# Decode attention over two caches: PV on four column groups, and V in one slot of a whole tile

## The chip, the cores and the metric

The kernel runs on one core of one Trainium2 chip. The metric is the device time of one execution in microseconds (us); several executions are timed, and the median counts. A profile is one more execution with the hardware profiler on.

## The reference

Two independent attention layers decode one token each and are joined side by side. Both have 32 heads of 128 and a cache of 16384 positions; layer A attends to all of them, layer B to the last 4096.

```python
q = (x @ wq).reshape(1, 1, 32, 128).transpose(0, 2, 1, 3)
k, v = k_cache, v_cache                      # B: only [:, :, Sk - 4096 :, :]
scores = einsum("bhqd,bhkd->bhqk", q, k) * 128 ** -0.5
o = einsum("bhqk,bhkd->bhqd", softmax(scores), v)
out = o.transpose(0, 2, 1, 3).reshape(1, 1, 4096) @ wo     # wo: 4096 x 512
return concatenate([out_A, out_B], axis=-1)                # 1 x 1 x 1024, bf16
```

x is 1 x 512, wq 512 x 4096, everything in bf16. A's K and V are 134 MB each, B's windows 33.5 MB each, the four weight matrices 4.2 MB each: 352 MB are read once.

## The kernel before

**Tiles.** A tile holds 8.39 MB of K: 128 partitions with 64 KB each. For A that is two heads: 64 partitions a head, 256 consecutive positions a partition. For B it is two groups of four heads (halves of a tile): a group has 32 partitions a head and 128 positions a partition. There are 20 tiles in a fixed list `steps`; B's are numbers 0, 7, 13 and 19, the rest are A's. T counts tiles, and a step is what the loop does for one tile; u is the half of a tile, CH = 128 positions.

**Scores on DVE.** `scores_prod` (L206) multiplies half a tile of K by q in place, 128 x 16384 elements. `scores_tree` folds the 128 products of a position with four additions (L213, 64 + 32 + 16 + 8 wide) and a reduction over the last 8 (L219) into `sc`. `unit_max` (L224, L226) takes the maximum per partition and turns it on PE; `max_all` (L231 to L238) takes the maximum per head and spreads it again over the partitions by a product on PE.

**Softmax on ACT.** `soft` makes the bias (L243), the exponentials with their sums (L246), and spreads p by head with a mask (L254), so that `pm` holds for four positions of a partition one column for each pair of head and position. `soft_sum` adds over the partitions on PE (L268, L273), `recip` inverts on DVE.

**PV on PE.** `pv` (L298): for each four positions of a partition one matmul with `pm` (128 x 8 for A, 128 x 16 for B) as weights and 128 x 512 of V as the moving operand. All add into the first 8 or 16 rows of one PSUM tile `o`; only the blocks where position meets position are wanted. `evict` scales by the reciprocal (L314, ACT), `columns` picks the wanted blocks with four small products (L329) and writes the heads' columns into `s.O` (L333). The last of A's tiles but one (`split`) and B's last tile use `pv_columns` instead (L344): V as weights, one matmul a position.

**Ends.** `project_q` (L183) makes q at the start. `permute_o` rearranges a side's columns, `project_out_rows` (L379) multiplies A's by wo, and `project_out_columns` (L393) B's, with wo in five pieces of 16, 8, 4, 3 and 1 rows.

**Order.** The schedule is written by hand; each engine runs its instructions in the order in which the program gives them. All large loads go through SP's queue in program order, and a load that waits for its slot holds those behind it. K has two slots of a whole tile (`kring`), V two of half a tile (`vring`, 32 KB a partition). At the start B's wq, half of K(0), A's wq, the other half and K(1) are loaded; the wq's sit in V's slots; x of both sides comes over ACT's queue into a corner of K's second slot. For half u of tile T the loop does this:

```python
if u == 0 and T >= 1:
    load_v(T - 1, 0)
    if T + 1 < NT:
        new_k(T + 1)
        load_k(T + 1)
```

then `columns`, `scores_prod(T, u)`, and where a softmax is due `max_all`, `soft` and `soft_sum`; for u == 0 then `pv(T - 2, 1)`, `load_v(T - 1, 1)` and `pv(T - 1, 0)`; then `scores_tree`, `recip`, `evict`, `unit_max`. So a tile's V is loaded during the next tile's scores, its first half ahead of K(T + 1) in SP's queue and its second half behind it, and the second half of PV runs a step later still. In the last two halves A's wo and B's last V go into K's free slot, B's wo into one of V's.

Of the kernel before, what the change touches and what calls it, by code (L numbers as in the profile page):

```python
# [25 lines left out]
def kernel(  # L26
# [26 lines left out]
    vring = ctx.enter_context(tc.tile_pool(name="vring", bufs=2))  # L53
# [4 lines left out]
    ps_o = ctx.enter_context(tc.tile_pool(name="ps_o", bufs=2, space=bass.MemoryType.PSUM))  # L58
# [5 lines left out]
    def vslot(name):  # L64
        return vring.tile([P, CH, DH], BF16, tag="vring", name=name)
# [9 lines left out]
    for s, n, x, wq, wo, nh in ((A, "A", A_x, A_wq, A_wo, 2), (B, "B", B_x, B_wq, B_wo, 4)):  # L75
        s.n, s.x, s.wq, s.wo, s.nh = n, x, wq, wo, nh
# [5 lines left out]
        s.rows = singles.tile([P, nh, 4], F32, tag=f"rows{n}", name=f"rows{n}")  # L82
# [42 lines left out]
    def load_v(T, u, dst=None):  # L125
        s, g = steps[T]
        V[T, u] = vslot("vt") if dst is None else dst
        if s is A:
            src = a_pair(A_v_cache, g)[:, u * CH : (u + 1) * CH, :].rearrange("p l d -> p (l d)")
        else:  # L130
            src = b_window(B_v_cache, 2 * g + u)
        nc.sync.dma_start(out=V[T, u][:, :, :].rearrange("p l d -> p (l d)"), in_=src)

    def load_wq(s):
        s.wq_t = vslot("wqt")
        nc.sync.dma_start(  # L136
            out=s.wq_t[:, :, :].rearrange("p a b -> p (a b)").rearrange("p (c f) -> p c f", c=KC),
            in_=s.wq.rearrange("(p c) f -> p c f", c=KC),
        )
# [9 lines left out]
    def make_masks(s):  # L149
        nc.vector.tensor_reduce(out=s.mask[:, :], in_=by_head(s, identf[:, :]), axis=AX.X, op=ALU.add)  # L150
        nc.vector.tensor_copy(s.rows[:, :, :], s.mask[:, :].unsqueeze(2).broadcast_to([P, s.nh, 4]))
# [22 lines left out]
    def project_q(s):  # L174
        wq = s.wq_t[:, :, :].rearrange("p a b -> p (a b)").rearrange(
# [13 lines left out]
    class Unit:  # L189
        def __init__(self, T, u):  # L190
            self.T = T
            self.s, g = steps[T]
            self.col = self.s.nh * g if self.s is A else self.s.nh * (2 * g + u)
            self.n = 2 * CH if self.s is A else CH
            self.rows = 4 * self.s.nh
            self.split = T == NT - 3
            self.last = self.split or T == NT - 1
            self.sc = one.tile([P, 2 * CH], F32, tag="sc", name="sc")

# [8 lines left out]
    def scores_tree(T, u):  # L208
        s, g = steps[T]
# [5 lines left out]
        if s is B or u == 0:  # L215
            units[T, u] = Unit(T, u)
        un = units[T, u if s is B else 0]
        c0 = u * CH if s is A else 0
        nc.vector.tensor_reduce(out=un.sc[:, c0 : c0 + CH], in_=k[:, :, 0:8], axis=AX.X, op=ALU.add)  # L219
        return un if s is B or u == 1 else None  # L220

    def unit_max(un):
        m = small.tile([P, 1], F32, tag="m", name="m")
        nc.vector.tensor_reduce(out=m[:, :], in_=un.sc[:, 0 : un.n], axis=AX.X, op=ALU.max)  # L224
        un.sm = ps_m.tile([P, 512], F32, tag="sm", name="sm")
        nc.tensor.transpose(un.sm[0:1, 0:P], m[:, :], identf[:, :])  # L226

    def max_all(un):
        s = un.s
        M = small.tile([1, 4], F32, tag="M", name="M")  # L230
        nc.vector.tensor_reduce(  # L231
            out=M[:, 0 : s.nh], in_=by_head(s, un.sm[0:1, 0:P]), axis=AX.X, op=ALU.max
        )
        Mr = one.tile([1, P], F32, tag="Mr", name="Mr")
        nc.vector.tensor_copy(  # L235
            by_head(s, Mr[:, :]), M[:, 0 : s.nh].unsqueeze(2).broadcast_to([1, s.nh, P // s.nh])
        )
        nc.tensor.matmul(un.sm[:, 128:129], lhsT=Mr[:, :], rhs=one_f[:, :], start=True, stop=True)  # L238

    def soft(un):  # L240
        s = un.s
        bias = small.tile([P, 1], F32, tag="bias", name="bias")
        nc.scalar.activation(out=bias[:, :], in_=un.sm[:, 128:129], func=ACT.Copy, scale=-inv)  # L243
        p = one.tile([P, 2 * CH], BF16, tag="p", name="p")
        cs = small.tile([P, 1], F32, tag="cs", name="cs")
        nc.scalar.activation(  # L246
            out=p[:, 0 : un.n], in_=un.sc[:, 0 : un.n], func=ACT.Exp, scale=inv, bias=bias[:, :],
            accum_out=cs[:, :],
        )
        un.cs = cs  # L250
        pm = small.tile([P, 4 * CH], BF16, tag="pm", name="pm")
        un.pm = pm[:, 0 : un.n * s.nh].rearrange("p (i h c) -> p i h c", h=s.nh, c=4)
        for j in range(s.nh):
            nc.scalar.activation(  # L254
                out=un.pm[:, :, j, :], in_=p[:, 0 : un.n].rearrange("p (i c) -> p i c", c=4),
                func=ACT.Copy, scale=s.mask[:, j : j + 1],
            )

        if un.last:
            un.csm = small.tile([P, 4], F32, tag="csm", name="csm")  # L260
            nc.scalar.activation(
                out=un.csm[:, 0 : s.nh], in_=s.mask[:, :], func=ACT.Copy, scale=un.cs[:, :]
            )

    def soft_sum(un):
        s = un.s
        if un.last:
            nc.tensor.matmul(  # L268
                un.sm[:, 136 : 136 + s.nh], lhsT=ones_col[:, :].broadcast_to([P, P]),
                rhs=un.csm[:, 0 : s.nh], start=True, stop=True,  # L270
            )
        else:
            nc.tensor.matmul(  # L273
                un.sm[0 : un.rows, 136:137], lhsT=s.rows[:, :, :].rearrange("p a b -> p (a b)"),
                rhs=un.cs[:, :], start=True, stop=True,
            )

    def recip(un):
        un.r = small.tile([P, 4], F32, tag="r", name="r")
        if un.last:  # L280
            nc.vector.reciprocal(un.r[:, 0 : un.s.nh], un.sm[:, 136 : 136 + un.s.nh])
        else:
            nc.vector.reciprocal(un.r[0 : un.rows, 0:1], un.sm[0 : un.rows, 136:137])  # L283

    ready = []

    def pv(T, u):
        s = steps[T][0]
        un = units[T, u if s is B else 0]
        if un.split and u == 1:  # L290
            pv_columns(un, V[T, u], u * CH // 4)
            return
        first, final = (True, True) if s is B or un.split else (u == 0, u == 1)
        if first:
            un.o = ps_o.tile([16, 512], F32, tag="o", name="o")
        i0 = u * CH // 4 if s is A else 0
        for i in range(CH // 4):
            nc.tensor.matmul(  # L298
                un.o[0 : un.rows, :],
                lhsT=un.pm[:, i0 + i, :, :].rearrange("p a b -> p (a b)"),  # L300
                rhs=V[T, u][:, 4 * i : 4 * i + 4, :],
                start=(first and i == 0),
                stop=(final and i == CH // 4 - 1),
            )
        if final and not un.split:
            ready.append(un)

    evicted = []

    def evict():  # L310
        while ready:
            un = ready.pop(0)
            un.osb = one.tile([16, 512], F32, tag="o4", name="o4")
            nc.scalar.activation(  # L314
                out=un.osb[0 : un.rows, :], in_=un.o[0 : un.rows, :], func=ACT.Copy,
                scale=un.r[0 : un.rows, 0:1],
            )
            evicted.append(un)
            if ready:
                columns()  # L320

    def columns():
        while evicted:
            un = evicted.pop(0)
            s, n = un.s, un.rows
            oc = ps_s.tile([P, 4], F32, tag="sp", name="oc")
            sel = identf[0:n, 0:n].rearrange("k (h c) -> k c h", c=4)
            for j in range(4):
                nc.tensor.matmul(  # L329
                    oc[:, 0 : s.nh], lhsT=un.osb[0:n, j * P : (j + 1) * P], rhs=sel[:, j, :],  # L330
                    start=(j == 0), stop=(j == 3),
                )
            nc.scalar.copy(s.O[:, un.col : un.col + s.nh], oc[:, 0 : s.nh])  # L333

    def evict_part(un):
        un.part = one.tile([16, 512], F32, tag="o4", name="o4p")
        nc.scalar.copy(un.part[0 : un.rows, :], un.o[0 : un.rows, :])

    def pv_columns(un, V_t, i0):
        s, n = un.s, un.rows  # L340
        part = getattr(un, "part", None)
        o = ps_o.tile([P, 4], F32, tag="o", name="ocol")
        for l in range(CH):
            nc.tensor.matmul(  # L344
                o[:, 0 : s.nh], lhsT=V_t[:, l, :], rhs=un.pm[:, i0 + l // 4, :, l % 4],
                start=(l == 0), stop=(part is None and l == CH - 1),
            )
# [182 lines left out]
```

## Time and profile before

| | |
|---|---|
| median of 3 runs | 827.29 us (827.22 to 827.47) |
| the profiled execution | 827.69 us, its span 825.8 us |
| DVE busy | 761.7 us, 92% |
| PE busy with matmuls / weight loads | 391.3 us / 173.0 us |
| ACT busy | 67.1 us |
| bytes read | 352.32 MB |

The span is what the profiler's records cover; the execution's own time lies 1.9 us above it. Lines such as L298 are lines of the kernel before. In the views, "idle before" is time in which an engine waited, and behind the arrow stands what ended the wait. A DMA view of a stretch counts the packets that the 16 DMA engines moved in it, the megabytes, and the packets' time as a share of 16 engines for the stretch's length. PE is matrix multiplication, PEld its weight loads, SPq the queue of the engine that issues the large loads.

### The profile page before, as it was taken

What the parts mean: (1) busy time and instruction counts of PE and PEld (TensorE: products, weight loads), DVE (VectorE), ACT (ScalarE), POOL (GpSimd) and SP (SyncE); (2) the same over time, 40 slices, a digit from 0 to 9 for tenths busy, and PEclk for the clock granted to TensorE, in tenths of its full rate; (3) what the DMA queues carried; (4) which work ended last, traced back from release to release, by engine and by line L of the source; (5) the groups of instructions that cost most, each with busy time, mean ns of one, the idle gap of its engine ahead of it and who ended that gap; (6) DMA issues with size and microseconds to landing.
All of it is one profiled execution on the core that took longest, in us unless ns stands there. A gap on an engine that the chain in (4) does not pass through costs nothing.

```text
span 825.8 us, 5009 instructions
## 1 busy us (share of the span) xinstructions
PE 391.3 (47%) x2107; PEld 173.0 (21%) x2107; DVE 761.7 (92%) x361; ACT 67.1 (8%) x194; POOL 0.7 (0%) x6
## 2 busy tenths in 40 slices
PE   3505062808172644537180817354553617181794
PEld 1201020303031212212030302121221203030444
DVE  1899999999999999999999999999999999999930
ACT  0111010101000001101010100010010101010120
POOL 0000000000000000000000000000000000000000
PEclk9766576868585858677675859585767767575685
DMA  9999999999999999999999999999999999999996
GB/s 383 436 432 445 423 448 417 447 416 439 432 427 432 429 436 429 439 424 438 424 443 422 445 418 430 437 427 441 421 443 424 447 417 447 416 432 432 426 432 287
DMA packets 10404, 352.64 MB, mean 427 GB/s; under 512 B 1163, under 2 KB 1294, under 8 KB 1550
## 3 DMA queue, kind: packets, MB, share of 16 engines
q1 hardware_dynamic: 10376, 352.33, 99.2%
q8 instruction: 16, 0.26, 0.1%
q14 instruction: 6, 0.05, 0.0%
q10 hardware_dynamic: 6, 0.00, 0.0%
HBM read 352.32 MB, written 0.00 MB: 427 GB/s over the span
## 4 chain that ended last, share of the span: by engine, by line
DVE 77%; DMA 20%; PE 2%; issue 1%; SPq 0%; ACT 0%; DVEq 0%
DVE kt L206 35%; DVE kt L213 34%; DMA kt<-in_A_k_cache_dram 10%; DVE sc L219 5%; DMA kt<-in_B_k_cache_dram 5%; DMA wot<-in_B_wo_dram 4%; DMA vt<-in_A_v_cache_dram 2%; PE o L298 1%; DVE m L224 1%; DVE Mr L235 1%; DVE M L231 0%; PE ocol L344 0%; DVE r L283 0%; SPq L136 0%; SPq L146 0%
## 5 line engine op out<-in xcount | busy, mean ns | idle before, releaser
L213 DVE TENSOR_TENSOR kt<-kt 128x8192 bf16<-128x8192 bf16 (+3 forms) x160 | 344.9, 2156 | 4.7
L298 PE MATMUL o<-vt,pm 128*8 128x512 bf16 (+1 forms) x1184 | 300.1, 420 | 0.8 <-DMA vt<-in_A_v_cache_dram 0.8
L206 DVE TENSOR_TENSOR kt<-kt,qA 128x16384 bf16<-128x16384 bf16 x32 | 277.5, 8672 | 3.1 <-DMA kt<-in_A_k_cache_dram 3.0
L298 PEld LDWEIGHTS <-pm 128*8 128x8 bf16 (+1 forms) x1184 | 110.2, 94 | 181.5 <-issue 60.8
L226 PE MATMUL sm<-identf,m 128*1 128x128 f32 x24 | 8.5, 355 | 199.6 <-DVE m L224 199.5
L238 PE MATMUL sm<-one_f,Mr 1*128 1x1 f32 x48 | 13.1, 340 | 177.2 <-DVE Mr L235 177.2
L206 DVE TENSOR_TENSOR kt<-kt,qB 128x16384 bf16<-128x16384 bf16 x8 | 69.5, 8684 | 14.6 <-DMA kt<-in_B_k_cache_dram 14.6
L219 DVE TENSOR_REDUCE sc<-kt 128x128 f32<-128x1024 bf16 x40 | 48.8, 1220 | 3.3 <-DVE kt L213 0.5
L238 PEld LDWEIGHTS sm<-one_f,Mr 1*128 1x128 f32 x48 | 11.1, 285 | 184.1 <-DVE Mr L235 183.7
L226 PEld LDWEIGHTS sm<-identf,m 128*1 128x1 f32 x24 | 1.9, 79 | 202.2 <-issue 193.3
L243 ACT ACTIVATE bias<-sm 128x1 f32<-128x1 f32 x24 | 4.1, 171 | 404.0 <-PE sm L238 403.9
L314 ACT ACTIVATE o<-o,r 8x512 f32<-8x512 f32 (+1 forms) x21 | 14.3, 679 | 158.0 <-PE o L298 158.0
L329 PE MATMUL oc<-identf,o 8*128 8x2 f32 (+1 forms) x168 | 22.0, 249 | 2.9 <-ACT o L314 2.9
L329 PEld LDWEIGHTS oc<-identf,o 8*128 8x128 f32 (+1 forms) x168 | 20.2, 186 | 10.4 <-issue 6.5
L254 ACT ACTIVATE pm<-p,maskA 128x256 bf16<-128x256 bf16 x32 | 14.5, 500 | 0.5
L183 PE MATMUL qp<-wqt,xbA 128*128 128x512 bf16 x32 | 8.8, 444 | 9.5 <-DMA wqt<-in_A_wq_dram 9.5
L183 PE MATMUL qp<-wqt,scratch 128*128 128x512 bf16 x32 | 10.0, 488 | 5.3 <-DMA wqt<-in_B_wq_dram 5.3
L359 DVE TENSOR_TENSOR OB<-ocol,r 128x4 bf16<-128x4 f32 x2 | 0.3, 163 | 13.1 <-PE ocol L344 13.1
L246 ACT ACTIVATE p<-sc,bias 128x256 bf16<-128x256 f32 (+1 forms) x24 | 11.3, 472 | 0.8
L333 ACT CAST OA<-oc 128x2 bf16<-128x2 f32 x15 | 2.4, 161 | 102.6 <-PE oc L329 102.6
L254 ACT ACTIVATE pm<-p,maskB 128x128 bf16<-128x128 bf16 x32 | 10.2, 390 | 0.3
L224 DVE TENSOR_REDUCE m<-sc 128x1 f32<-128x256 f32 (+1 forms) x24 | 9.0, 374 | 0.6
(69 smaller groups left out, 98.6 us busy)
## 6 DMA issues: line engine op xcount, KB each, us to landing
vt<-in_A_v_cache_dram SPq DMA_DIRECT2D x32, 4096.0 KB, 26.5
kt<-in_B_k_cache_dram SPq DMA_DIRECT2D x8, 4096.0 KB, 35.3
vt<-in_B_v_cache_dram SPq DMA_DIRECT2D x7, 4096.0 KB, 33.2
wqt<-in_B_wq_dram SPq DMA_DIRECT2D x1, 4096.0 KB, 12.6
wqt<-in_A_wq_dram SPq DMA_DIRECT2D x1, 4096.0 KB
wot<-in_A_wo_dram SPq DMA_DIRECT2D x1, 4096.0 KB
wot<-in_B_v_cache_dram SPq DMA_DIRECT2D x1, 4096.0 KB, 29.3
wot<-in_B_wo_dram SPq DMA_DIRECT2D x1, 2048.0 KB, 26.9
```

Source lines behind the costliest of these rows:

```text
L183: nc.tensor.matmul(qp[:, :, :], lhsT=s.xb[:, j, c, :], rhs=wq[:, c, j, g : g + 4, :], start=(k == 0), stop=(k == n - 1),)
L206: nc.vector.tensor_tensor(out=k, in0=k, in1=s.q[:, j : j + 1, :].broadcast_to([P, CH, DH]), op=ALU.mult)
L213: nc.vector.tensor_tensor(out=k[:, :, 0:w], in0=k[:, :, 0:w], in1=k[:, :, w : 2 * w], op=ALU.add)
L219: nc.vector.tensor_reduce(out=un.sc[:, c0 : c0 + CH], in_=k[:, :, 0:8], axis=AX.X, op=ALU.add)
L224: nc.vector.tensor_reduce(out=m[:, :], in_=un.sc[:, 0 : un.n], axis=AX.X, op=ALU.max)
L226: nc.tensor.transpose(un.sm[0:1, 0:P], m[:, :], identf[:, :])
L238: nc.tensor.matmul(un.sm[:, 128:129], lhsT=Mr[:, :], rhs=one_f[:, :], start=True, stop=True)
L246: nc.scalar.activation(out=p[:, 0 : un.n], in_=un.sc[:, 0 : un.n], func=ACT.Exp, scale=inv, bias=bias[:, :], accum_out=cs[:, :],)
L254: nc.scalar.activation(out=un.pm[:, :, j, :], in_=p[:, 0 : un.n].rearrange("p (i c) -> p i c", c=4), func=ACT.Copy, scale=s.mask[:, j : j ...
L298: nc.tensor.matmul(un.o[0 : un.rows, :], lhsT=un.pm[:, i0 + i, :, :].rearrange("p a b -> p (a b)"), rhs=V[T, u][:, 4 * i : 4 * i + 4, :], ...
L314: nc.scalar.activation(out=un.osb[0 : un.rows, :], in_=un.o[0 : un.rows, :], func=ACT.Copy, scale=un.r[0 : un.rows, 0:1],)
L329: nc.tensor.matmul(oc[:, 0 : s.nh], lhsT=un.osb[0:n, j * P : (j + 1) * P], rhs=sel[:, j, :], start=(j == 0), stop=(j == 3),)
```

## The change

- V has one slot of a whole tile (64 KB a partition). A's V comes in one load of 128 rows of 64 KB; B's still in two halves. Both wq's sit in the two halves of this slot at the start.
- `pv` spreads the matmuls over four blocks of 32 PSUM rows: `s.o` has 128 rows, matmul i of a group goes to rows 32 * (i % 4) and on (A), or to one of two blocks for each group of heads (B). `evict` reads all 128 rows, `columns` picks with a selector `s.sel` that sums over the blocks. `s.o` is one PSUM tile a side, cleared at the start.
- B is treated by whole tile: one maximum, softmax and PV for both groups of four heads.
- A step now has its whole `pv(T - 1)` behind the softmax of T - 1, and the loop's loads are V(T - 1), whole, and K(T + 1). The `split` tile is gone; A's last tile takes the same way as the others.
- At the end `permute_o(A)` and `project_out_rows(A)` stand ahead of the last maxima, and the second half of the last `pm` is spread by DVE. A's wo and the first half of B's last V go into K's free slot, the second half and B's wo into V's slot.
- x of each side comes in three loads (a quarter, a quarter, a half) instead of one.
- The eight DMA semaphores are handed out in turn, and with six loads of x ahead SP's third and fourth load (A's wq, the second half of K(0)) now wait for x's first and second.

```diff
-    vring = ctx.enter_context(tc.tile_pool(name="vring", bufs=2))
+    vring = ctx.enter_context(tc.tile_pool(name="vring", bufs=1))
...
-    ps_o = ctx.enter_context(tc.tile_pool(name="ps_o", bufs=2, space=bass.MemoryType.PSUM))
+    ps_o = ctx.enter_context(tc.tile_pool(name="ps_o", bufs=1, space=bass.MemoryType.PSUM))
...
-        return vring.tile([P, CH, DH], BF16, tag="vring", name=name)
+        return vring.tile([P, 2 * CH, DH], BF16, tag="vring", name=name)
...
+        s.sel = singles.tile([P, s.parts, nh * 4], F32, tag=f"sel{n}", name=f"sel{n}")
+        s.o = ps_o.tile([P, 512], F32, tag=f"o{n}", name=f"o{n}")
...
-    def load_v(T, u, dst=None):
+    def load_v(T):
         s, g = steps[T]
-        V[T, u] = vslot("vt") if dst is None else dst
+        V[T] = vslot("vt")
         if s is A:
-            src = a_pair(A_v_cache, g)[:, u * CH : (u + 1) * CH, :].rearrange("p l d -> p (l d)")
+            nc.sync.dma_start(
+                out=V[T][:, :, :].rearrange("p l d -> p (l d)"),
+                in_=a_pair(A_v_cache, g).rearrange("p l d -> p (l d)"),
+            )
         else:
-            src = b_window(B_v_cache, 2 * g + u)
-        nc.sync.dma_start(out=V[T, u][:, :, :].rearrange("p l d -> p (l d)"), in_=src)
+            for u in (0, 1):
+                load_v_half(T, u, V[T][:, u * CH : (u + 1) * CH, :])
...
+    def pv(un):
+        s, n, G = un.s, un.n // 4, un.s.groups
+        for i in range(n):
+            for v in range(s.parts):
+                r0 = 32 * (v * G + i % G)
+                l = v * n + i
                 nc.tensor.matmul(
+                    s.o[r0 : r0 + un.rows, :],
+                    lhsT=un.pm[:, l, :, :].rearrange("p a b -> p (a b)"),
+                    rhs=V[un.T][:, 4 * l : 4 * l + 4, :],
+                    start=(i < G), stop=(i >= n - G),
                 )
+
+    def evict(un):
+        un.osb = one.tile([P, 512], F32, tag="o4", name="o4")
+        nc.scalar.activation(out=un.osb[:, :], in_=un.s.o[:, :], func=ACT.Copy, scale=un.r[:, 0:1])
...
-            nc.scalar.dma_start(out=s.x_row, in_=s.x[0, 0:1, :])
+            for a, b in ((0, D // 4), (D // 4, D // 2), (D // 2, D)):
+                nc.scalar.dma_start(out=s.x_row[:, a:b], in_=s.x[0, 0:1, a:b])
...
+        for T in range(NT):
+            if T >= 1:
+                load_v(T - 1)
                 if T + 1 < NT:
                     new_k(T + 1)
                     load_k(T + 1)
+            if T == NT - 1:
                 W = kslot("wot")
                 load_wo(A, W[:, 0:CH, :], (HQ,))
+                load_v_half(T, 0, W[:, CH : 2 * CH, :])
+            scores_prod(T, 0)
+            if T >= 1:
+                un = units[T - 1]
+                max_all(un)
+                soft(un)
+                spread_p(un)
+                soft_sum(un)
+                pv(un)
+            scores_tree(T, 0)
+            if T >= 1:
+                recip(un)
+                evict(un)
+                columns(un)
+            scores_prod(T, 1)
+            scores_tree(T, 1)
+            if T < NT - 1:
+                unit_max(units[T])
+        Z = vslot("wot")
+        load_v_half(NT - 1, 1, Z[:, 0:CH, :])
+        load_wo(B, Z[:, CH : 2 * CH, :], wo_pieces)
+        un = units[NT - 1]
         permute_o(A)
         project_out_rows(A)
+        unit_max(un)
+        max_all(un)
+        soft(un)
+        spread_p(un, 0, CH)
+        spread_p(un, CH, 2 * CH, nc.vector.tensor_scalar_mul)
+        soft_sum(un)
+        recip(un)
+        pv_columns(un, 0, W[:, CH : 2 * CH, :])
+        pv_columns(un, 1, Z[:, 0:CH, :])
         permute_o(B)
         project_out_columns(B, wo_pieces)
```

More of the change, by code (lines that the diff above doesn't have):

```diff
@@ L228, in max_all @@
     def max_all(un):
[L229 to L232, printed above, removed]
-        )
[L234 to L253, printed above, removed]
+        s, n = un.s, un.s.parts
@@ new lines, in max_all @@
+        nc.vector.tensor_reduce(out=Mv, in_=rows, axis=AX.X, op=ALU.max)
+        if s is A:
+            nc.vector.tensor_copy(wide, Mv.unsqueeze(2).broadcast_to([1, s.nh, P // s.nh]))
+        else:
+            nc.vector.tensor_copy(wide, Mv.unsqueeze(3).broadcast_to([1, n, s.nh, P // s.nh]))
+        for v in range(n):
+            nc.tensor.matmul(
+                un.sm[:, 256 + v : 257 + v], lhsT=Mr[:, v * P : (v + 1) * P], rhs=one_f[:, :],
+                start=True, stop=True,
+            )
@@ L254, in soft @@
+    def soft(un):
+        s, n = un.s, un.n
+        bias = small.tile([P, 2], F32, tag="bias", name="bias")
+        nc.scalar.activation(
+            out=bias[:, 0 : s.parts], in_=un.sm[:, 256 : 256 + s.parts], func=ACT.Copy, scale=-inv
+        )
+        un.p = one.tile([P, 2 * CH], BF16, tag="p", name="p")
+        un.cs = small.tile([P, 2], F32, tag="cs", name="cs")
+        for v in range(s.parts):
             nc.scalar.activation(
-                out=un.pm[:, :, j, :], in_=p[:, 0 : un.n].rearrange("p (i c) -> p i c", c=4),
@@ L261, in soft, with on_scalar @@
-            nc.scalar.activation(
-                out=un.csm[:, 0 : s.nh], in_=s.mask[:, :], func=ACT.Copy, scale=un.cs[:, :]
-            )
+            un.csm = small.tile([P, 8], F32, tag="csm", name="csm")
+            for v in range(s.parts):
+                nc.scalar.activation(
+                    out=un.csm[:, v * s.nh : (v + 1) * s.nh], in_=s.mask[:, :], func=ACT.Copy,
+                    scale=un.cs[:, v : v + 1],
+                )
+    def on_scalar(out, in_, mask):
+        nc.scalar.activation(out=out, in_=in_, func=ACT.Copy, scale=mask)
@@ L273, in soft_sum @@
             nc.tensor.matmul(
-                un.sm[0 : un.rows, 136:137], lhsT=s.rows[:, :, :].rearrange("p a b -> p (a b)"),
-                rhs=un.cs[:, :], start=True, stop=True,
+                un.sm[v * w : (v + 1) * w, 264:265], lhsT=s.rows[:, :, :, :].rearrange("p r a b -> p (r a b)"),
+                rhs=un.cs[:, v : v + 1], start=True, stop=True,
             )
     def recip(un):
[L279 to L303, printed above, removed]
-            )
-        if final and not un.split:
-            ready.append(un)
@@ L308 @@
[L308 to L316, printed above, removed]
-            )
[L318 to L347, printed above, removed]
-        if part is not None:
-            sel = identf[0:n, 0:n].rearrange("k (h c) -> k c h", c=4)
-            for j in range(4):
-                nc.tensor.matmul(
-                    o[:, 0 : s.nh], lhsT=part[0:n, j * P : (j + 1) * P], rhs=sel[:, j, :],
-                    start=False, stop=(j == 3),
-                )
-        un.ocol = o
@@ L359, in scale_columns, with pv_columns @@
+    def pv_columns(un, v, V_t):
+        s = un.s
+        oc = ps_s.tile([P, 4], F32, tag="sp", name="ocol")
+        for l in range(un.n):
+            nc.tensor.matmul(
+                oc[:, :], lhsT=V_t[:, l, :], rhs=un.pm[:, (v * un.n + l) // 4, :, l % 4],
+                start=(l == 0), stop=(l == un.n - 1),
+            )
         nc.vector.tensor_tensor(
-            out=s.O[:, un.col : un.col + s.nh], in0=un.ocol[:, 0 : s.nh], in1=un.r[:, 0 : s.nh], op=ALU.mult
+            out=s.O[:, un.col(v) : un.col(v) + s.nh], in0=oc[:, :],
+            in1=un.r[:, v * s.nh : (v + 1) * s.nh], op=ALU.mult,
```

172 lines of the change are left out of this document (84 added, 88 removed).

## The prediction

> **What bounds the kernel now.** I read the page first: the share of each engine, the DMA row and the chain that ended last.
>
> ```profile
> span 825.8 us, 5009 instructions
> PE 391.3 (47%) x2107; PEld 173.0 (21%) x2107; DVE 761.7 (92%) x361; ACT 67.1 (8%) x194; POOL 0.7 (0%) x6
> ...
> DMA  9999999999999999999999999999999999999996
> ...
> q1 hardware_dynamic: 10376, 352.33, 99.2%
> q8 instruction: 16, 0.26, 0.1%
> ...
> DVE 77%; DMA 20%; PE 2%; issue 1%; SPq 0%; ACT 0%; DVEq 0%
> ```
>
> The chain names DVE for 77% of the span, but DVE is not what sets the end. SP's queue (q1) keeps the 16 DMA engines busy for 99.2% of 825.8, 819.2 us; the other 6.6 us are the start before the first load and the output behind the last. A program whose transfers never pause ends earlier only if they get shorter or their edges do. DVE must be held against that step by step, which the next rows do: from the chain in order of time, two DVE products a tile apart and the two long waits for K; from SP's timeline, when K and V are issued.
>
> ```profile
> 157.40 8.60 DVE kt L206
> ...
> 195.53 8.60 DVE kt L206
> ...
> 596.89 39.91 DMA kt<-in_A_k_cache_dram
> ...
> 674.62 40.38 DMA kt<-in_A_k_cache_dram
> ...
> 137.90 0.33 SPq L114 DMA_DIRECT2D kt<-in_A_k_cache_dram  x1
> 157.79 7.24 SPq L132 DMA_DIRECT2D vt<-in_A_v_cache_dram  x2
> 176.04 0.33 SPq L114 DMA_DIRECT2D kt<-in_A_k_cache_dram  x1
> ...
> q1 hardware_dynamic: 8344, 301.83, 100.1%
> ...
> q1 hardware_dynamic: 507, 1.56, 56.5%
> ```
>
> The last two rows are the DMA view of 100 to 800 us and of 816 to 823 us. A step of DVE takes 195.53 - 157.40 = 38.13 us. A step of DMA moves K and V of one tile, 16.78 MB; at 301.83 MB in 700 us (431.2 GB/s) that is 38.9 us. So DMA is slower by 0.8 us a step, and late in the run DVE waits for K. A tile of K (8.39 MB, 19.5 us) lands 40 us after its issue: about 20 us of V stands ahead of it in the queue, so the engines never look for work.
>
> **The 64 KB rows.** Counting descriptors: 72 loads by SP, of which 16 (A's K) have 128 rows of 64 KB and make 2048 packets if a row is one packet; everything else makes 7168, completions 72 x 16 = 1152, the output 8. The sum is 10376, the page's number, so a 64 KB row does travel as one packet. A's V is now 32 loads of 128 rows of 32 KB; afterwards 16 loads of 128 rows of 64 KB: 2048 data packets and 256 completions fewer, q1 should count 8072. The price of a packet comes from the two windows above, one with large packets and one where B's wo goes in small ones. 8344 packets and 301.83 MB took 1.001 x 700 x 16 = 11211 us of engine time; 507 packets and 1.56 MB took 0.565 x 7 x 16 = 63.3 us. Solved together: 36.8 us a MB and 11.5 ns a packet. 2048 x 11.5 ns / 16 engines = 1.5 us, with the completions 1.65 us; 0.01 MB of rounding in the small window moves the price by 0.8 ns. I take **1.4 us**; the ends are 0 (a packet's price hides in the next one's) and 1.8.
>
> **One V slot, and PV in four groups.** V(T) may now be issued only when the whole PV of T-1 has read the slot; before, half a tile waited for half. In the queue V(T) stands behind K(T+1), which takes 19.5 us after V(T-1) has landed. PV(T-1) and the issue must fit into that, or the engines stand still. SP is in order: what is queued behind V(T)'s wait is K(T+2), which cannot go before K(T) is consumed anyway.
>
> ```profile
> 0.74 0.52 ACTq L414 DMA_DIRECT2D scratch<-in_B_x_dram  x1
> 1.29 0.21 ACTq L414 DMA_DIRECT2D scratch<-in_A_x_dram  x1
> 2.02 0.21 PEld L156 LDWEIGHTS <-scratch 1*128 1x128 bf16 x4 [2.02 <-DMA scratch<-in_B_x_dram]
> 7.83 0.20 PEld L156 LDWEIGHTS <-scratch 1*128 1x128 bf16 x4 [5.59 <-DMA scratch<-in_A_x_dram]
> 23.13 8.69 DVE L206 TENSOR_TENSOR kt<-kt,qB 128x16384 bf16<-128x16384 bf16 x1 [14.29 <-DMA kt<-in_B_k_cache_dram]
> ...
> 72.65 9.40 PE L298 MATMUL o<-vt,pm 128*16 128x512 bf16 x32
> ...
> 727.32 16.65 PE L298 MATMUL o<-vt,pm 128*8 128x512 bf16 x64
> ...
> L298 PE MATMUL o<-vt,pm 128*8 128x512 bf16 (+1 forms) x1184 | 300.1, 420 | 0.8 <-DMA vt<-in_A_v_cache_dram 0.8
> L298 PEld LDWEIGHTS <-pm 128*8 128x8 bf16 (+1 forms) x1184 | 110.2, 94 | 181.5 <-issue 60.8
> ```
>
> A full tile is 64 matmuls. One after another they took 16.65 us. No row shows groups beside each other, so the bounds are 16.65 / 4 = 4.2 us and 64 x 0.42 = 26.9 us (every matmul at its mean duration, none overlapped). I take 16 rounds of four at 0.42 us, 6.7 us: the groups have separate rows of weights and of output, and PE is cold after its pause. An issue (0.33 us) and the landing of a small load on an empty queue (2.02 - 0.74 = 1.3 us) come on top. PV may thus take up to 19.5 - 1.6 = 17.8 us before a gap opens in the transfers; even 16.65 us fits. Cost in the steps: nothing, hidden by K.
>
> A rule to weigh: the 72.65 row runs 32 load-matmul pairs in 9.40 us, 294 ns a pair, less than the matmul's mean alone, so weight loads (94 ns) already hide. [...]
>
> **V ahead of K.** The queue's order changes from V half, K, V half to whole V, K. Each K lands 4.19 MB, 9.7 us, later, so DVE's head start is gone from the second tile and it waits about 0.8 us in every step. That costs nothing until the end, where DVE finishes later.
>
> **The end.** Rows of the tail:
>
> ```profile
> 753.18 8.68 DVE L206 TENSOR_TENSOR kt<-kt,qB 128x16384 bf16<-128x16384 bf16 x1
> 790.20 0.68 ACT L314 ACTIVATE o<-o,r 8x512 f32<-8x512 f32 x1 [5.37 <-PE o L298]
> 791.63 0.28 DVE L224 TENSOR_REDUCE m<-sc 128x1 f32<-128x128 f32 x1
> 792.06 0.27 PE L226 MATMUL sm<-identf,m 128*1 128x128 f32 x1
> 793.36 8.75 PE L379 MATMUL out_row<-wot,OpA 128*1 128x512 bf16 x32
> 793.42 0.17 ACT L243 ACTIVATE bias<-sm 128x1 f32<-128x1 f32 x1
> 794.15 1.28 ACT L254 ACTIVATE pm<-p,maskB 128x128 bf16<-128x128 bf16 x4
> ...
> 802.55 3.46 PE L344 MATMUL ocol<-pm,vt 128*128 128x4 bf16 x128
> 812.27 3.57 PE L344 MATMUL ocol<-pm,wot 128*128 128x4 bf16 x128 [6.26 <-DMA wot<-in_B_v_cache_dram]
> ...
> 817.27 0.81 PE L393 MATMUL out_cols<-OpB,wot 128*128 128x1 bf16 x25 [0.27 <-ACT OpB L374]
> 821.98 0.59 PE L393 MATMUL out_cols<-OpB,wot 128*128 128x1 bf16 x16 [0.46 <-DMA wot<-in_B_wo_dram]
> ```
>
> B's last half of V landed at 812.27; 1.4 earlier is 810.9. Counting back 9.7 us for each 4.19 MB: first half of that V 801.1, A's wo 791.4, V(18) 781.7, K(19) 762.2, K(18) 723.3. DVE: 723.3 + 38.1 + (791.63 - 753.18) = 799.9, then the maxima. PE, in order, has A's output product ahead of their transposes: V(18) at 781.7, 0.3, PV 6.7, from the eviction to the product 793.36 - 790.20 = 3.2, product 8.75: 800.7. From the transposes to the bias took 1.36 us, with the second half's rows some 2.1; from the bias to the end of the spread 2.0, with a second exponential and two column sums 3.0; a column product 3.5. So the first half's columns end at 809.3, before 810.9: hidden by the last V. The second half then ends 1.4 earlier than before, at 814.4, and B's output, paced by the last pieces of wo, too. Both column products had to wait before; the spare is 810.9 - 809.3 = 1.6 us, and 1.2 more behind, because the output's 128 matmuls (4.2 us busy) end at 820.0 while the last piece allows 821.2.
>
> **Edits without a price.** B by whole tile halves its maxima, sums and reciprocals (under 2 us of DVE, off the path since DVE waits). Clearing both outputs and the selectors costs DVE some 2 us inside the 14.29 us it idles before 23.13. x in six loads in place of two delays its last piece: the second 1 KB took 6.5 us behind traffic. Queued together I expect under 20 us, which delays the first product by a few us; DVE, faster by 0.8 us a step, wins back up to 14. One behind another at 6.5 us each would leave a gap of about 3 us after the fourth load; that is the far end. SP's third and fourth load now wait for x's first two pieces, with 19 us of transfers queued ahead.
>
> **The sum.** The profiled execution took 827.69 (span 825.8); minus 1.4 is 826.3. The median of the runs is 0.4 below it, 827.29, and becomes **825.9**. 0.2%, about what a measurement of this kernel can tell from no change, is 1.65 us: the gain lies just inside.
>
> **Rivals.** *More from the packets:* 1.65 with the completions, and PE's program is some 200 instructions shorter, which may spare the slowest engine one of the sixteen 16 KB instruction loads (0.6 us): 825.0. Against: each such load goes to one engine only. *Loads in series (slower):* if the four groups' weight loads hide neither behind matmuls nor behind each other, PV takes 16 x (4 x 0.094 + 0.42) = 12.7 us; no gap in the steps, but at the end the product with A's wo starts late. PV is free there up to 6.7 + 1.6 + 1.2 = 9.5 us, then it costs us for us: 12.7 - 9.5 = 3.2 later, less 1.4: 829.1. [...] *No overlap of the groups at all:* PV at 16.65 gives 827.3 + 7.15 - 1.4 = 833.0, again by the end alone; it decides from a PV of 12.6 us on. Were PV cold throughout, 26.9 us, 18 loads would each open 9.1 us, near 990. For it: no trace here shows groups together; against: 294 ns pairs. *The rows are cut in two anyway:* 827.3; the count above speaks against it.
>
> **How the numbers follow.** Forecast 0.55 (825.2 to 826.8), more from the packets 0.20, loads in series 0.07, no overlap 0.10, rows cut or a small loss in the start or tail 0.08. The range 825.0 to 830.0 takes in the serial loads and leaves out the full absence of overlap and a little below. Faster: 0.20 and 0.08 of the forecast's lower edge, 0.28; slower 0.07 + 0.10 + 0.08 = 0.25; same 0.47.
>
> **What would show it.** Right: q1 at 8072 packets and still 99% busy; DVE waiting for K in nearly every step, by about 0.8 us; PV of a tile at 5 to 9 us; the last column product at about 810.9. Wrong: zeros in the DMA row, SP waiting for PV longer than K lasts, PV above 10 us, or the transposes of the last maxima behind A's output product past 803.

## The result, and the profile after

The changed kernel takes 825.86 us (median of 19 runs, 825.66 to 826.25), the kernel before 827.28 (19 runs, 827.05 to 827.54). The ratio is 0.9983, with a 95% interval of 0.9976 to 0.9990: 1.4 us less. The profiled execution of the changed kernel took 825.66, its span is 823.9. Lines named from here on are those of the changed kernel; an experiment that adds a line shifts them by one or two.

The page after: the busy time of the engines, the DMA row, the queues, the chain that ended last and three groups (busy and mean of one, then idle before and what ended it).

```profile
span 823.9 us, 4724 instructions
PE 202.7 (25%) x1985; PEld 100.7 (12%) x1985; DVE 763.9 (93%) x353; ACT 60.1 (7%) x168; POOL 0.7 (0%) x6
...
DMA  9999999999999999999999999999999999999997
...
q1 hardware_dynamic: 8072, 352.33, 99.2%
q8 instruction: 15, 0.25, 0.1%
...
DMA 82%; PE 15%; DVE 1%; SPq 0%; issue 0%; ACTq 0%; ACT 0%; DVEq 0%
...
L227 DVE TENSOR_TENSOR kt<-kt,qA 128x16384 bf16<-128x16384 bf16 x32 | 277.8, 8683 | 11.0 <-DMA kt<-in_A_k_cache_dram 10.9
L331 PE MATMUL oA<-vt,pm 128*8 128x512 bf16 x1024 | 92.3, 538 | 132.1 <-DMA vt<-in_A_v_cache_dram 132.1
...
L331 PEld LDWEIGHTS <-pm 128*8 128x8 bf16 (+1 forms) x1216 | 37.3, 111 | 216.7 <-issue 196.3
```

PE's busy time fell by half, from 391.3 to 202.7 us, and the program by 285 instructions. Neither is where the 1.4 us come from: SP's queue is busy for 99.2% of the span, as before, with the same 352.33 MB, and the span is shorter, as the first experiment will show, because the queue has 2304 packets fewer. DVE has become 2 us longer and lost its place in the chain, where it stood for 77% and now stands for 1%. In its place stands DMA with 82%, which is what the queue's share had said of the kernel before already.

The timeline of the tail of the changed kernel (start, length, engine, line; in brackets how long the engine had been idle and what ended it):

```profile
703.70 6.04 PE L331 MATMUL oA<-vt,pm 128*8 128x512 bf16 x64 [8.13 <-DMA vt<-in_A_v_cache_dram]
709.78 0.33 SPq L132 DMA_DIRECT2D vt<-in_A_v_cache_dram  x1
...
723.19 8.69 DVE L227 TENSOR_TENSOR kt<-kt,qA 128x16384 bf16<-128x16384 bf16 x1 [0.63 <-DMA kt<-in_A_k_cache_dram]
...
742.57 5.38 PE L331 MATMUL oA<-vt,pm 128*8 128x512 bf16 x64 [8.13 <-DMA vt<-in_A_v_cache_dram]
...
761.00 0.33 SPq L157 DMA_DIRECT2D wot<-in_A_wo_dram  x1
...
781.38 6.45 PE L331 MATMUL oA<-vt,pm 128*8 128x512 bf16 x64 [8.79 <-DMA vt<-in_A_v_cache_dram]
...
791.10 8.46 PE L383 MATMUL out_row<-wot,OpA 128*1 128x512 bf16 x32 [0.28 <-DMA wot<-in_A_wo_dram]
...
799.16 0.42 DVE L244 TENSOR_REDUCE m<-sc 128x2 f32<-128x256 f32 x1
...
799.73 0.38 PE L249 MATMUL sm<-identf,m 128*1 128x128 f32 x2 [0.17 <-DVE m L244]
...
804.34 3.55 PE L358 MATMUL ocol<-pm,wot 128*128 128x4 bf16 x128 [0.78 <-ACT pm L297]
...
810.55 3.58 PE L358 MATMUL ocol<-pm,wot 128*128 128x4 bf16 x128 [2.66 <-DMA wot<-in_B_v_cache_dram]
...
820.24 0.58 PE L397 MATMUL out_cols<-OpB,wot 128*128 128x1 bf16 x16 [0.44 <-DMA wot<-in_B_wo_dram]
```

PV of a tile, 64 matmuls, takes 4.9 to 6.5 us over the whole trace where a tile took 16.65, and SP issues the next V as soon as it ends (703.70 + 6.04 = 709.74, then 709.78). Thirteen microseconds later K is there, and DVE has waited 0.63 us for it. At the end both products that set the time still wait for DMA: the last half of B's V at 810.55 (before 812.27), the last piece of wo at 820.24 (before 821.98), both 1.7 us earlier.

### The profile page after: what moved, and what is told of

Its sections match the earlier page's. It is cut to its first block, busy times and chain, and to the rows that moved or that the text cites. A ratio compares the mean times of both kernels' runs of the same rounds, so it can differ in the third digit from the quotient of the medians.

```text
span 823.9 us, 4724 instructions
## 1 busy us (share of the span) xinstructions
PE 202.7 (25%) x1985; PEld 100.7 (12%) x1985; DVE 763.9 (93%) x353; ACT 60.1 (7%) x168; POOL 0.7 (0%) x6
## 3 DMA queue, kind: packets, MB, share of 16 engines
q1 hardware_dynamic: 8072, 352.33, 99.2%
## 4 chain that ended last, share of the span: by engine, by line
DMA 82%; PE 15%; DVE 1%; SPq 0%; issue 0%; ACTq 0%; ACT 0%; DVEq 0%
DMA vt<-in_A_v_cache_dram 65%; DMA vt<-in_B_v_cache_dram 13%; PE oA L331 11%; DMA wot<-in_B_wo_dram 4%; PE oB L331 2%; PE qp L203 2%; DMA scratch<-in_A_x_dram 2%; DVE kt L227 1%; SPq L141 0%; ACTq L419 0%; SPq L157 0%; PE out_cols L397 0%; ACT qB L207 0%; PE out_rows L407 0%; DVE rows L409 0%
## 5 line engine op out<-in xcount | busy, mean ns | idle before, releaser
L331 PE MATMUL oA<-vt,pm 128*8 128x512 bf16 x1024 | 92.3, 538 | 132.1 <-DMA vt<-in_A_v_cache_dram 132.1
L331 PEld LDWEIGHTS <-pm 128*8 128x8 bf16 (+1 forms) x1216 | 37.3, 111 | 216.7 <-issue 196.3
L276 ACT ACTIVATE bias<-sm 128x1 f32<-128x1 f32 (+1 forms) x20 | 3.4, 172 | 420.8 <-PE sm L268 420.8
L340 ACT ACTIVATE o<-oA,r 128x512 f32<-128x512 f32 x16 | 11.0, 688 | 220.5 <-PE oA L331 220.5
L331 PE MATMUL oB<-vt,pm 128*16 128x512 bf16 x192 | 17.2, 494 | 20.3 <-DMA vt<-in_B_v_cache_dram 16.2
L348 PE MATMUL oc<-selA,o 128*128 128x2 f32 x128 | 16.9, 254 | 12.7 <-ACT o L340 12.7
L348 PEld LDWEIGHTS oc<-selA,o 128*128 128x128 f32 x128 | 15.5, 191 | 20.8 <-ACT o L340 20.8
L315 PE MATMUL sm<-cs,rowsA 128*128 128x1 f32 x32 | 9.4, 362 | 14.3 <-ACT p L282 14.3
L315 PEld LDWEIGHTS sm<-cs,rowsA 128*128 128x128 f32 x32 | 8.0, 310 | 15.7 <-ACT p L282 15.7
```

Of the source, the lines that this page charges most:

```text
L315: nc.tensor.matmul(un.sm[v * w : (v + 1) * w, 264:265], lhsT=s.rows[:, :, :, :].rearrange("p r a b -> p (r a b)"), rhs=un.cs[:, v : v + 1] ...
L331: nc.tensor.matmul(s.o[r0 : r0 + un.rows, :], lhsT=un.pm[:, l, :, :].rearrange("p a b -> p (a b)"), rhs=V[un.T][:, 4 * l : 4 * l + 4, :], ...
L340: nc.scalar.activation(out=un.osb[:, :], in_=un.s.o[:, :], func=ACT.Copy, scale=un.r[:, 0:1])
L348: nc.tensor.matmul(oc[:, 0:w], lhsT=un.osb[:, j * P : (j + 1) * P], rhs=sel[:, j, :], start=(j == 0), stop=(j == 3),)
```

## The experiments

All start from the changed kernel. Three questions: does the time follow the packets, does it follow PV, and does DVE matter? A fourth came of the first: can B's loads have 64 KB rows too?

**A's V in two loads of 32 KB rows, or four of 16 KB.** Nothing else differs.

```diff
-            nc.sync.dma_start(out=V[T][:, :, :]..., in_=a_pair(A_v_cache, g)...)
+            w = 2 * CH // 2                       # the other kernel: 2 * CH // 4
+            for c in range(2):                    # range(4)
+                nc.sync.dma_start(out=V[T][:, c * w : (c + 1) * w, :]...,
+                                  in_=a_pair(A_v_cache, g)[:, c * w : (c + 1) * w, :]...)
```

> A's V goes into the same one slot, but in two loads of 128 rows of 32 KB. Theory (the gain is the price of packets): 2048 data packets and 256 completions more than the changed kernel, 8072 becomes 10376, and the time goes back to that of before, 827.2 to 827.5 us, with the DMA engines still 99% busy. Rival (the gain comes from elsewhere: one instruction load fewer for PE, the order of V and K, fewer small operations): 825.9 us, or part of the way (826.5 if the instruction load gave 0.6).

> A's V in four loads of 128 rows of 16 KB. Theory: 6144 data packets and 768 completions more than the changed kernel, 14984 in all; at 11.5 ns on 16 engines that is 4.4 us from the data packets and 5.0 with the completions: 830.2 to 830.9 us. Rival (packets cost nothing, or only down to 32 KB): 827.4 us or less.

Measured: 827.08 us with two loads (11 runs, 826.87 to 827.58; ratio to the kernel before 0.9997, interval 0.9989 to 1.0006) and 829.89 with four (6 runs, 829.58 to 830.19; 1.0031, 1.0018 to 1.0043). SP's queue, on the pages of the two:

```profile
q1 hardware_dynamic: 10376, 352.33, 99.2%
```

```profile
q1 hardware_dynamic: 14984, 352.33, 99.3%
```

Same bytes, same share, more packets, more time. From 8072 to 10376 packets the time grows by 1.22 us, 1.22 x 16 / 2304 = 8.5 ns of an engine's time for each; from 10376 to 14984 by 2.81, 9.8 ns. The price is a rough one: the intervals are 0.7 to 1.0 us to either side. Two loads of 32 KB bring back all but 0.2 us of the gain, so the cutting of V's rows is the cause, and neither PV nor the queue's new order. A row cut in two is also one load more a tile; no run has the one without the other. The 0.2 us between this kernel and the one before stays open: its interval takes in no difference.

**PV in one column group, in two, and in a mixture.** The matmuls are the same 64 a tile; only the rows of PSUM to which they add differ.

```diff
-                r0 = 32 * (v * G + i % G)
+                r0 = 32 * v * G                       # one group
+                r0 = 32 * (v * G + i % (G // 2))      # two of A's four
+                g = i % (G // 2) if i < n // 2 else 0 # mixed: half on two, half on one
+                r0 = 32 * (v * G + g)
```

> The changed kernel with all matmuls of a PV in one group of columns (A: output rows 0 to 7 only; B: one group for each half). Theory (the groups run beside each other in the changed kernel, PV 5.4 to 6.5 us a tile of A): PV 16 to 18 us a tile; that still fits under K's 19.5 us, so the steps stay as they are and the DMA row shows no gap; at the end PV, the columns and the product with A's wo run late and hold up the last maxima on PE: about 6 us, 832 us in all. Rival 1 (the groups bring nothing, weights loaded beside matmuls do it): PV stays at 6 us, 825.9. Rival 2 (V's slot is short already): the DMA engines pause in each step, some 18 times 1 to 10 us, 845 to 1000 us.

> A's matmuls on two of the four groups (B's on one for each half). Theory (PV is free up to about 9.5 us): PV of a tile of A some 8 to 9 us, and the time unchanged, 825.7 to 826.2. Rival (PV's length sits on the path through V's one slot, us for us): 2 to 3 us more for each of 18 loads, over 860.

> The first half of a tile's matmuls on two of the four groups, the second half on one (B's on one for each half), so that PV of a tile of A takes 12 to 13 us. Theory (up to about 14 us no gap opens in the transfers, and at the end PV is free up to 10 us and then costs us for us): the DMA row without a gap, 828 to 829 us. Rival 1 (gaps open as soon as PV is over 10 us): 832 us or more with pauses in the DMA engines. Rival 2 (the end has more to spare): 825.9.

Two groups: 825.78 us (11 runs, 825.61 to 828.04; 0.9988, 0.9979 to 0.9997), the same as four in the median. Three of the eleven runs took 827.7 to 828.0 us; no trace of such a run was kept, so what they lost stays open. Mixed: 828.93 (8 runs, five of them at 828.58 to 828.96 and three, with the profiled one, at 830.17 to 830.83; 1.0024, 1.0014 to 1.0034), 3.1 more. One group: 843.73 (4 runs, 842.90 to 848.15; 1.0209, 1.0187 to 1.0231), 17.9 more, where about 832 was expected. The PV of one tile on the timelines of two groups, then of the mixture with the transposes of the last maxima:

```profile
742.61 9.34 PE L331 MATMUL oA<-vt,pm 128*8 128x512 bf16 x64 [8.14 <-DMA vt<-in_A_v_cache_dram]
```

```profile
703.90 12.95 PE L332 MATMUL oA<-vt,pm 128*8 128x512 bf16 x64 [8.13 <-DMA vt<-in_A_v_cache_dram]
716.88 0.33 SPq L132 DMA_DIRECT2D vt<-in_A_v_cache_dram  x1
...
723.37 8.69 DVE L227 TENSOR_TENSOR kt<-kt,qA 128x16384 bf16<-128x16384 bf16 x1 [0.61 <-DMA kt<-in_A_k_cache_dram]
...
761.18 0.33 SPq L157 DMA_DIRECT2D wot<-in_A_wo_dram  x1
...
781.56 13.37 PE L332 MATMUL oA<-vt,pm 128*8 128x512 bf16 x64 [8.79 <-DMA vt<-in_A_v_cache_dram]
...
798.17 8.45 PE L384 MATMUL out_row<-wot,OpA 128*1 128x512 bf16 x32 [0.28 <-ACT OpA L379]
...
806.55 0.38 PE L249 MATMUL sm<-identf,m 128*1 128x128 f32 x2
```

With two groups PV of a tile is 2 to 4 us longer, and nothing comes of it in the median. With the mixture the steps still run on time: A's wo is issued at 761.18, with four groups at 761.00. The cost is at the end: PV of A's last tile ends 7.1 us later (781.56 + 13.37 = 794.93 against 787.83), the product with A's wo starts at 798.17 instead of 791.10, and behind it the transposes of the last maxima at 806.55 instead of 799.73, with nothing in brackets: PE comes late to data that had been there. The prediction's "free up to 9.5 us, then us for us" gives 13.37 - 9.5 = 3.9 us for this execution; it took 830.19, 4.5 more than that of the changed kernel, and the medians differ by 3.1.

With one group the other half of the prediction, that the steps are free up to 17.8 us, fails. The DMA views of 100 to 760 us, first of the changed kernel, then of one group; below it DVE's waits for K in one group (total, times, longest) and a step of it on the timeline:

```profile
DMA packets 5624, 285.22 MB, mean 432 GB/s; under 512 B 622, under 2 KB 622, under 8 KB 622
...
q1 hardware_dynamic: 5610, 285.02, 100.0%
```

```profile
DMA packets 5415, 278.89 MB, mean 423 GB/s; under 512 B 594, under 2 KB 594, under 8 KB 594
...
q1 hardware_dynamic: 5401, 278.69, 98.7%
```

```profile
DVE kt L227 <- DMA kt<-in_A_k_cache_dram: 24.6, 16, 4.4
```

```profile
637.46 15.88 PE L331 MATMUL oA<-vt,pm 128*8 128x512 bf16 x64 [8.13 <-DMA vt<-in_A_v_cache_dram]
653.37 0.33 SPq L132 DMA_DIRECT2D vt<-in_A_v_cache_dram  x1
...
656.80 8.69 DVE L227 TENSOR_TENSOR kt<-kt,qA 128x16384 bf16<-128x16384 bf16 x1 [0.48 <-DMA kt<-in_A_k_cache_dram]
...
697.49 8.69 DVE L227 TENSOR_TENSOR kt<-kt,qA 128x16384 bf16<-128x16384 bf16 x1 [2.45 <-DMA kt<-in_A_k_cache_dram]
```

And an earlier step of the same trace:

```profile
493.39 0.33 SPq L132 DMA_DIRECT2D vt<-in_A_v_cache_dram  x1
...
497.26 8.69 DVE L227 TENSOR_TENSOR kt<-kt,qA 128x16384 bf16<-128x16384 bf16 x1 [0.93 <-DMA kt<-in_A_k_cache_dram]
```

In those 660 us 6.3 MB fewer were moved, 14.7 us at 432 GB/s, and the queue is no longer full: 98.7% instead of 100.0% are 8.6 us. V is issued at 653.37, 3.4 us ahead of K's last byte (656.80 is when DVE could begin), and still time is lost: 697.49 - 656.80 = 40.7 us for this step instead of 38.9. The start and length of every single packet in this trace show why. Some of the 16 engines run dry before the last of them has finished K: until 653.5 us each holds a packet, at 654.0 us only 4 do, from 657.0 us on all 16 again, and K's last packet ends at 656.28. V's first packets behind the gap take 2.8 to 3.7 us instead of 2.42, which goes with the rest of the 14.7 us. Among A's steps whose product waits for K, those with V issued 3.7 us or less ahead of that product have such a gap, and those with 3.9 us (493.39 to 497.26) or more have none. The mixture's issue (716.88 to 723.37) is 6.5 us ahead, and neither its trace nor that of the changed kernel or of two groups has a gap between 100 and 760 us.

**x in one load a side, as before.**

```diff
-            for a, b in ((0, D // 4), (D // 4, D // 2), (D // 2, D)):
-                nc.scalar.dma_start(out=s.x_row[:, a:b], in_=s.x[0, 0:1, a:b])
+            nc.scalar.dma_start(out=s.x_row, in_=s.x[0, 0:1, :])
```

> x of each side in one load again. Theory (x is hidden: the first product may start up to some 10 us later without reaching the end): the first product starts 0.8 us earlier, at 23.1 us, and the time is that of the changed kernel, 825.7 to 826.1 us. Rival (the three pieces matter, by the turn of the DMA semaphores or by traffic at the start): over 0.4 us away from 825.9, to either side.

Measured: 826.08 us (11 runs, 825.74 to 826.45; 0.9984, 0.9976 to 0.9993), 0.2 above the changed kernel with overlapping runs. The first product on the timelines, of the changed kernel and then of this one:

```profile
23.89 8.69 DVE L227 TENSOR_TENSOR kt<-kt,qB 128x16384 bf16<-128x16384 bf16 x1 [6.31 <-ACT qB L207]
```

```profile
22.83 8.69 DVE L227 TENSOR_TENSOR kt<-kt,qB 128x16384 bf16<-128x16384 bf16 x1 [14.06 <-DMA kt<-in_B_k_cache_dram]
```

In three pieces q comes after K and DVE starts 1.1 us later, and that costs nothing at the end. Whether the 0.2 is real stays open.

**A shorter DVE.** The widest of the four folding additions of the scores is left out: the folding starts at a quarter of the products' width instead of half of it.

```diff
-        w = DH // 2
+        w = DH // 4
```

> The first of the four folding additions (128 x 8192) is left out of all 40 half tiles: only half of the products of a position enter its score. DVE has 40 x 4.4 = 177 us less to do. Theory (the transfers set the time, DVE waits for K): DVE waits 9 us more in each step and the time stays, 825.5 to 826.2 us. Rival (DVE at 93% busy sets the time): 100 us or more less.

Measured: 825.86 us (10 runs, 825.62 to 826.08; 0.9982, 0.9973 to 0.9991), the median of the changed kernel to the digit. Its page's engine line and DVE's longest sum of waits:

```profile
PE 199.9 (24%) x1985; PEld 100.5 (12%) x1985; DVE 587.1 (71%) x313; ACT 60.1 (7%) x168; POOL 0.7 (0%) x6
```

```profile
DVE kt L227 <- DMA kt<-in_A_k_cache_dram: 167.0, 16, 19.1
```

DVE does 177 us less and waits 156 us more for K. It isn't the bound, although it is busy for 93% and the chain of the kernel before named it for 77%.

**B in rows of 64 KB as well.** One tile of B as one group of eight heads, 16 partitions a head: the loads have 1 x 64 KB for each partition, as A's have. The edit is longer than the line shown: B's softmax and PV take eight heads at once, and some small buffers are given up for room.

```diff
-        return cache[0, 4 * g : 4 * g + 4, SkB - WB : SkB, :].rearrange("h (i l) d -> i h (l d)", l=CH)
+        return cache[0, 8 * g : 8 * g + 8, SkB - WB : SkB, :].rearrange("h (i l) d -> i h l d", l=2 * CH)
```

> B's K and V too in rows of 64 KB: a tile is one group of eight heads with 16 partitions a head and 256 positions a partition, in one load (the first K and the last V stay in two halves of 32 KB rows). 768 data packets and 96 completions fewer than the changed kernel, 7208. Theory (9 to 11.5 ns a packet over 16 engines): 0.5 to 0.6 us less than the changed kernel, 825.2 to 825.4 us, unless the later last tile of K (whole instead of in halves) uses up the spare at the end. Rival (rows of 64 KB pay for A alone, since B's rows lie interleaved by head): 825.9 or more.

Measured: 1009.24 us (5 runs, 1007.66 to 1035.42; 1.2198, 1.2178 to 1.2218). Its page (GB/s by slice), and the DMA view of 330 to 345 us, in the middle of one of B's loads:

```profile
GB/s 292 291 335 250 245 420 423 451 422 436 433 425 344 209 357 384 208 308 433 428 440 422 438 357 209 328 417 208 285 433 433 431 433 436 383 208 292 339 215 220
...
q1 hardware_dynamic: 7208, 352.33, 99.3%
```

```profile
DMA packets 49, 3.16 MB, mean 211 GB/s; under 512 B 0, under 2 KB 0, under 8 KB 0
...
q1 hardware_dynamic: 48, 3.15, 100.6%
```

The packets fell as planned, the queue is still full, and each packet of B takes twice as long: 208 to 211 GB/s where A's go at 432. B's 67 MB at half the rate are some 160 us more, most of the 183. Two things are new in these loads: the source's rows jump by 4 MB from head to head, and the 128 rows are written as 16 x 8, partition index outermost. Three runs take them apart on A's V, one run each, beside 827.74 us for the kernel before:

```diff
-                in_=a_pair(A_v_cache, g).rearrange("p l d -> p (l d)"),
+                in_=a_pair(A_v_cache, g).rearrange("(r e) l d -> e r (l d)", e=16),  # rows 16 x 8
+                in_=a_pair(A_v_cache, g).rearrange("(r e) l d -> e r (l d)", e=32),  # rows 32 x 4
+            # halves: two loads, partitions 0 to 63 and 64 to 127, rows of 64 KB in order
```

> A's V in two loads of 64 partitions each, rows of 64 KB, one behind the other; 256 completions more, the same data packets. It asks why B's loads ran at half rate as 16 x 8 rows. Theory S (the writing side: at any time only half of SBUF's partition groups were written): here too all engines write into one half of the partitions, V at half rate, 16 x 19.5 us more, about 1137 us. Theory R (the reading side, or the form of the load): 826 us.

> A's V in one load whose source is written as 16 x 8 rows of 64 KB out of the same 8 MB (neighbours 64 KB apart, groups 1 MB apart), so that positions and heads land in other partitions than the products assume: the numbers that come out are those of other rows. Theory (the form 16 x 8 itself is slow, whatever the source): V at half rate, packets at about 5.1 us, some 1137 us. Rival (B's heads 4 MB apart are slow in rows of 64 KB): 826 us.

> The same with 32 x 4 rows (groups 2 MB apart), the form in which B's loads run at full rate with rows of 32 KB; again other rows than the products assume. Theory (16 x 8 alone is slow): packets at 2.42 us and 826 us. Rival (any interleaved source is slow once its rows are 64 KB): packets at about 5.1 us, some 1137 us.

Measured: halves 1300.38, 16 x 8 1289.96, 32 x 4 825.87 us. The GB/s rows of the pages of the halves, of 16 x 8 and of 32 x 4:

```profile
GB/s 404 436 445 208 344 196 323 220 315 202 317 200 318 213 361 425 208 310 196 291 200 309 174 283 202 248 273 420 202 279 220 287 174 283 176 240 266 195 280 220
```

```profile
GB/s 407 428 435 228 349 199 328 208 336 202 330 206 336 204 415 392 201 335 201 273 222 263 199 311 178 299 285 363 216 269 222 261 195 289 180 227 259 196 280 224
```

```profile
GB/s 385 436 431 434 447 423 443 433 433 437 426 443 423 424 439 443 414 452 420 447 414 452 418 445 413 450 426 420 440 442 430 430 436 426 437 421 444 420 429 294
```

Rows of 64 KB in another order go at the full rate if they are written as 32 x 4, and at about 200 GB/s as 16 x 8, with no source that jumps by 4 MB. The jump isn't the cause either way: in the changed kernel B's loads of 32 KB rows, written as 32 x 4, jump by 4 MB too, and no slice of that page between the first and the last is under 410 GB/s. So the form of the load is what is left. One thing more differs between the two runs and was not taken apart from the form: rows that follow each other lie 1 MB apart in the source of 16 x 8 and 2 MB apart in that of 32 x 4. A load that reaches 64 partitions alone is about as slow: slices of 174 to 220 in the first row, with faster ones between them where K goes. Half the rate is what theory S expected there; whether a limit on the writing side sets this rate, and whether a 16 x 8 load meets the same one, no run shows. Both kernels also cost more than half the rate alone (826 + 16 tiles x 19.5 us = 1138 us); on their pages SP's queue is full for only 92.7% and 92.8% of the span, which is about half of the rest, and what else there is was not followed. A window of 4096 positions has no 32 x 4 form with 64 KB rows (32 partitions a head make 32 KB), so B stays as it is, and no version found here is clearly faster than the changed kernel.

## Why the prediction was right, point by point

**What bounds it.** Right, and against the chain of waits: a DVE with 177 us less changes nothing, 2304 packets change the time by 1.2 us.

**The packets.** The count of 8072 came out exactly. The price, 11.5 ns from the window with small packets, agrees with the packets' own lengths: in the kernel with two loads, between 100 and 760 us, one of 64 KB takes 2.425 us and two of 32 KB 2 x 1.218 = 2.436, 11 ns more. But only 8.5 to 9.8 ns of it reach the kernels' time, and no run shows where the rest goes. The 1.4 us taken, less than the 1.65 that the price gives, is 1.22 by the rows alone; the rest of the 1.4 us measured is the open 0.2. So the term that carries the forecast was right to 0.2 us, and the agreement with the median, 825.9 against 825.86, is in part luck. The instruction load to which a rival gave 0.6 us did fall away (q8 counts 15 instead of 16), but it fell away in the kernel with two loads too, so it is worth at most the open 0.2.

**PV in four groups.** 4.9 to 6.5 us against 6.7. Loads in series, 12.7 us, did not happen: 64 pairs in 5.38 us are 84 ns a pair, less than the mean of one weight load (111 ns). Behind what they hide, no run tells. The prediction's "separate rows of weights" is wrong: each load is 128 x 8 (`128*8` on the page), all 128 rows in every group, and what the kernel keeps apart is the rows of PSUM. What it calls cold shows in the kernel before: PE worked 0.77 us between 718 and 727, and in the PV that starts at 727.32 the granted clock was 0.50 up to 732 us, at 586 to 631 ns a matmul, and 1.00 from 733 to 743, at 379 ns.

**The limit of one V slot.** Wrong, and without effect on the forecast: PV was to be free in the steps up to 17.8 us. One group at 15.4 to 16.5 us already loses some 14 us there, the mixture at 11.8 to 13.5 none. The step that failed is "19.5 - 1.6": the small load on an empty queue that gave 1.3 us is no measure of how far ahead of the queue's end a big load must be issued, because the engines don't finish together. It is between 3.7 and 3.9 us here, which leaves PV some 15.6 us. By it the rival without any overlap was priced at 833.0, and it is 843.7: it would have paid in the steps as well as at the end.

**V ahead of K.** Right; DVE's waits for K in the changed kernel (total, times, longest):

```profile
DVE kt L227 <- DMA kt<-in_A_k_cache_dram: 10.9, 15, 1.4
```

That is 0.7 us in each of 15 products with K of A and none with K of B; 0.8 in every step was predicted.

**The end.** Predicted and measured: last half of V 810.9 and 810.55; DVE's last maxima 799.9 and 799.16; transposes behind A's product 800.7 and 799.73; first half's columns finished 809.3 and 804.34 + 3.55 = 807.89; so spare 1.6 and 2.66. In the trace PE and DVE arrive there within 0.2 us of each other, as the count had them.

**x in three pieces.** The product waited for q instead of K, as expected, by 0.8 us more than before (23.89 against 23.13) rather than a few; DVE won it back. SP's fourth load did not wait for x's second piece: it waited 10.5 us for B's wq and was issued at 13.10 instead of 2.56, and the queue was still full for 98.7% of the time from 8 to 24 us (before, 99.1%).

## What to carry to other kernels

When a queue is full for 99% of the span, count its packets before anything else: halving the number of V's rows was worth nearly all that the change brought (1.22 of 1.4 us), while halving PE's busy time or taking a quarter of DVE's gave nothing by itself (827.08 us in the kernel with two loads, 825.86 with the shorter DVE). PE's column groups count in another way: with one slot for V the kernel loses 17.9 us without them. A slot that is refilled through a full queue has to be free before the first engine runs out of work, here almost 4 us ahead of the end of the load before it, so a budget that is "just enough" on paper should be tried with one kernel that uses it up. And of a load look at the form in which its partitions are written as well as at the length of its rows: the same 64 KB rows went at 430 or at 210 GB/s.

## What was not expected of the hardware

A load of 128 rows of 64 KB written as 16 x 8, and one of 64 partitions, ran at about 200 to 210 GB/s, and the same rows as 32 x 4 at 432. Two column groups took PV of a tile from 15.9 to 9.3 us (1.7 times) and four to 4.9 to 6.5 (2.4 to 3.2 times), though each of the 64 matmuls has its own weights to load. A packet more costs 8.5 to 9.8 ns of an engine by the kernels' times, with rows from 16 to 64 KB. And the 16 engines ended a load of 8.4 MB 2.7 us apart (653.6 to 656.3 us in the kernel with one group), so that the queue ran dry in part while its last load was still on the way.
